# A fused long-convolution and gated-unit backward kernel: every engine's hand-searched order replaced by another one, and one spectrum store issued earlier

## The chip, the cores and the metric

The kernel runs as one program on 1 core of a Trainium2 chip. A core has five engines that run side by side: TensorE (PE, matrix multiplication into the accumulator memory PSUM), VectorE (DVE) and ScalarE (ACT), which do the elementwise work and copy PSUM back to the on-chip memory SBUF, GpSimd (POOL), and SyncE (SP), which here issues nearly all DMAs. Each engine takes its own queue of instructions strictly in order, and waits where a semaphore says that an input isn't there yet. The metric is the device time of one execution, in microseconds (us); less is better.

## The reference

A forward and its gradient. The forward takes x (2048 tokens, 512 channels), normalises it to xn, convolves k with 4 taps, multiplies by v, convolves the product kv with a 2048-long kernel by FFT (length 4096), gates it with xn, and multiplies it by a gated unit with 1376 hidden columns:

```python
def _A_ref(q, k, v, shift_k, ssm_k, ssm_D):
    k_shift = sum(k_pad[:, t:t + S, :] * shift_k[:, ks - 1 - t] for t in range(ks))
    kv = k_shift * v
    y = irfft(rfft(pad(kv)) * rfft(pad(ssm_k)))[:S].astype(bfloat16)
    return q * (y + kv * ssm_D)

def _B_ref(x, w_gate, w_up, w_down):
    return (sigmoid(x @ w_gate) * (x @ w_up)) @ w_down

xn = _layernorm(x)
out = x + _A_ref(xn, k, v, shift_k, ssm_k, ssm_D) * silu(_B_ref(xn, w_gate, w_up, w_down))
```

Ten outputs are asked for: `out`, and for a given `grad_out` the gradients with respect to q, k, v, the 4 taps, `ssm_k` (512 x 2048, called the spectrum's gradient here, `out_5`), `ssm_D`, and the three weights (`out_7`, `out_8`, `out_9`). All is bfloat16 with f32 accumulation.

## The kernel before

The sequence is laid out as 128 partitions x 16 (`NJ`), the 512 channels in 4 groups (`NG`) of 128 for the convolution, and the tokens in 8 pairs of tiles (`NP`) for the gated unit. The code is written as generators, one for each stream of work. Forward: `strG` (gate and up products `gu_gen`, down product `z_gen`), `strK` and `strV` (the FFT of the long kernel and of kv), `strX` (product of the spectra and inverse). Backward: `strZ` (elementwise gradient of the gate), `strD` (`dh_gen`: gradient of the hidden columns; `x_gen`: gradient of xn, which multiplies by the transposed weights `WgT` and `WuT`), then `dW` (the three weight gradients), `frontC` and `backC` (the FFT of the gradient of y, the products with the stored spectra, and two inverses, channel group by channel group).

The FFT is made of two steps. `step1` and `inv1` are matmuls of the whole 128 x 128 array. `step2` and `inv2` are 32-point transforms: they cut the array into 16 pieces of 32 x 32, and one call of `step2` is 16 matmuls, one for each piece; `inv2` makes 32. A third form stands in `backC` (line 1442, "the strip" from here on): for the tap gradients each channel group makes 64 matmuls of 128 x 32 column strips, four strips side by side, all into one accumulator. In a profile the three forms are told apart as 128\*128, 32\*32 and 128\*32; in a list of instructions the output's shape tells them apart (128xN, 32x512 and 32x128). `last_rows` (line 1467) ends the program with five matmuls that leave 4 rows each (128\*4), and two tiny stores.

Nothing is issued while the generators run. `Rec` numbers and records every operation (`add`), 6,118 in all, with its dependences; `emit` (line 522) then issues them by the table `ORDER`: for each engine the list of operation numbers in the order of its queue ("4008+3" stands for 4008 to 4011), and in "moves" the order of all DMAs. An operation that may run on ACT or DVE (a copy out of PSUM, `evac`, or the normalisation in `ln`) runs on the engine whose list has its number. `BANKS` picks the PSUM banks of each accumulator. So each engine's order is written out by hand, down to the single matmul, and every instruction has one line in the profile, 527 (529 after the change), where it is emitted.

Places that matter below: operations 4008 to 4071 and 4631 to 4694 are the strips of channel groups 0 and 1; 5888 to 5891 and 5894 are the matmuls of `last_rows`. On SP, 2478 and 2484 load the transposed `w_gate` and `w_up` (`b_w2`, line 1138), in one DMA each that transposes on its way; 2476 loads a tile of `grad_out`; 5800 is the store of the last channel group's spectrum gradient (`out_5`, line 1437), 512 KB; 5982, 6049, 6083 and 6117 are stores of `out_8`; 5893 and 5896 are the tiny stores of `last_rows`.

Of the kernel before, what the change touches and what calls it, by code (L numbers as in the profile page):

```python
# [37 lines left out]
        943+1 340 458 945+5 341+2 854+7 344 882+7 414+15 397+1 461+7 509+5 399 515+1 712+5 545+7 567+3 563+2 718+1 566  # L38
        720+2 783+10 609+3 601+7 613+3 817+15 863+15 667+2 659 670+3 660+6 674 891+12 1203+6 1158+7 904+2 952+11 988+4
        964 983+2 979+3 986 965 1210 993+5 966+1 999+4 622+3 630+7 626+3 638+3 646+7 642+3 1044+3 1212+15 970+7 1048+3  # L40
        1035+7 1167+2 1089+7 1170+1 1006+7 1172+5 1016+15 1056+10 1100+15 1305+4 1240+15 755+1 751+2 747+3 754 757+5
        771 763 767+3 772+6 764+2 1310+10 1344+15 1190+7 1182+7 1389+14 1362+4 1404 1367+2 844+1 836+7 1429+1 1433+3
        846+2 1431 849+2 920+10 1432 931+4 1509+10 1121+31 1487+6 1338+3 1334+1 1494+3 1617 1336 1259+2 1337 1618+5
        1263+3 1624+8 1262 1235+3 1231+3 1540+15 1070+1 1078+3 1072+5 1082+3 1688+15 1636+7 1276+7 1268+7 1292+7
        1284+7 1644+7 1707+10 1416+7 1408+7 1789+3 1773+1 1439+15 1718+4 1372+15 1775+3 1793 1522+6 1504+2 1766+1 1529
        1500 1794 1501+1 1762+1 1503 1507 1764+1 1795+1 1768+1 1456 1460+3 1457+2 1779 1797+2 1531+7 1854+2 1780+3
        1857+12 1881+5 1568+1 1560+7 1570+5 1887+9 1908+15 1968+5 1828+7 1976+1 1819 1978 1820 1979+2 1974+1 1982+1
        1821+5 2022+10 1666+2 1674+7 1670+3 1669 2033+4 2040+7 1581+31 2139+2 2087+1 2147+5 1872+1 2142 1874+5 2143+3
        2089+4 2153+1 2051 1474+3 1470+1 1478+3 1466+3 1472+1 2052+5 2094+3 2058+3 1726+31 2157+15 1899+7 2192+13
        1837+12 1802+14 2206+1 1850+2 2210 1817 2211+14 1955+7 1947+7 2245+11 2287+2 2257+3 2290+4 2066+2 2074+6  # L50
        2069+1 2081 2071+2 2332+15 2301+3 1994+7 1986+7 2010+7 2002+7 2313+2 2305+2 2371+1 2316+7 2308+3 2373+4 2363+7
        2381+9 2378 2099+31 2391+5 2402+15 2420+9 2175 2236+3 2430+1 2240+3 2183 2228+7 2184 2432+3 2185+1 2176 2441+6
        2177+4 2187 2452 2464+2 2453+1 2182 2467+2 2279 2448 2455 2280+1 2456+3 2282 2188 2274+3 2189 2470+4 2190
        2460+1 2490+4 2462 2495+10 2510+5 2358+3 2353+2 2516 2518+5 2517 2356 2524+1 2485 2479+1 2530+11 2548+1 2486
        2637 2629+5 2638+4 2609+3 2617+6 2577 2613+1 2487 2615 2578 2550 2481 2579+3 2616 2635+1 2624 2583+1 2551+2
        2643+1 2488 2649 2554 2650+1 2482 2652+8 2585 2555+8 2586+6 2748+12 2564 2593 2761 2594+1 2762+1 2565+4 2596
        2704 2768 2705+1 2788 2707 2789 2597+1 2776+1 2790+1 2796 2769+1 2667+6 2797 2771+1 2778 2792+2 2674 2779+4
        2798+1 2675+6 2773+2 2682+4 2708+1 2687+1 2795 2710+14 2891 2883+2 2892+3 2903+1 2835 2905 2886 2906 2887 2725
        2896 2806+2 2888+1 2897+1 2911+4 2907+1 2836+1 2890 2809 2916+1 2838+1 2918 2909+1 2840+13 2923+2 2854 3014
        2926+3 2855+1 3022+4 3015 2810 2930+4 3016+3 2811+1 3020+1 2813+10 3027+2 2824+3 3042 3034+3 2970+8 2941 3062  # L60
        2942+1 3038 3054+2 3043+1 3039 3057+1 3063+1 2979 3045+1 3040 2980 3041 3065 3059 3047 2981 3048+1 2944+5
        3060+1 2982+1 3101 3072 2950+11 2984+4 3147+2 3175+1 3155+1 2989+2 3167+1 3150+1 3169 3152+1 3177+2 3170+3
        3154 3157+5 3073 3180 3174 3102+4 3181+1 3107+1 3074+1 3109+1 3187+1 3076+6 2962 3083+1 3189+8 3085 3322 3198
        3111+1 3086 3205 3113 3206 3274+2 3314 3087 3315 3277 3316 3282 3114 3088 3234+1 3283 3323+1 3115 3284+1 3089
        3317 3278 3207 3318 3090 3286 3279+1 3287 3091+2 3319+1 3288+1 3325 3321 3236 3281 3208 3237+1 3116+4 3294+15
        3209+3 3239+6 3332 3417 3213 3418 3246+1 3397 3425+2 3214 3405+2 3121+1 3248 3419 3333 3420+4 3398+1 3334+1
        3400 3428 3249 3401+3 3408+4 3429+3 3250 3361 3215 3251+1 3573 3253 3216 3574 3362+1 3254 3437+1 3364 3336+1
        3439+5 3217 3445+3 3365 3218+5 3338 3224+2 3366+1 3255 3751 3339+9 3569 3368+6 3575 3570 3528+1 3375+4 3576
        3380+2 3532+1 3822 3534+1 3571 3530 3572 3531 3349+4 3823 3455+8 3519 3547 3464 3543+3 3520 3824 3523 3521+1
        3548+2 3465+11 3825+3 3524+2 3487+21 3752+3 3673+8 3756 3587+7 3579+7 3682+1 3829 3552+7 3699+7 3691+7 3684+4  # L70
        3560+7 3830+7 3843 3757+5 3893+3 3610+7 3602+7 3763+2 3839 3844 3766 3845 3626+7 3618+7 3897+9 3840 3768 3846
        3813 3907 3769+3 3817+2 3814+1 3773 3820 3774+1 3816 3989+2 3908 3992+6 3637+31 3841+1 3999+4 3865+4 4004
        3870+2 4120+5 3714+15 3777+7 3738+7 3730+7 4085+14 4126+3 3793+3 3919+2 3797+3 3922+4 4100 4130+4 4148+1 4135
        3785+7 3915 3911+3 3916+2 3801+7 3848+5 4150+5 3882+2 3856+1 3854 3858 4156+2 3855 3885 3859+1 4078 4165+2
        3861+2 4159 3874+2 4160+3 4168 3943+1 4169 3935 3886+2 3877+4 4184+1 4074+3 4170+1 3889 4186+10 4079+2 4172
        3936 3945+3 3937+5 4173 3949+1 4174+2 3974+1 3982+3 3970+1 3978+1 3972+1 3980+1 3976+1 4177+3 4197+5 4111
        4115+1 4203+2 4106 4137+2 4141 4107 4507 4206 4142 4117 4143+1 4207+1 4508+2 4108 4209+2 4511+3 4118 4212
        4515+2 4140 4102 4112 4518+3 4213+2 4113 4103 4216 4114 4217+8 4104+1 4109 4522 4540+1 4226+12 3932 4542+8
        4239 4268+6 4280+3 4276+3 4008+3 4275 4296+1 4292+2 4298+1 4012+8 4288+2 4021+3 4295 4025+3 4291 4029+42
        4284+3 4240+7 4551+3 3952+10 4555 3963+4 4249+3 4580+15 4303+2 4311+5 4306+3 4317+1 4310 4327+4 4319+3 4332+1  # L80
        4323+3 4334 4700+4 4613 4705+7 4614 4344+11 4340+3 4713+2 4615+3 4719+7 4363+15 4383+1 4379+3 4387+1 4385
        4389+4 4386 4394 4727+7 4454+2 4619+9 4740+11 4458+1 4472+1 4752 4463 4753+1 4474+1 4755 4476 4802 4467+3 4457
        4460+1 4464+2 4803 4477+2 4949+3 4804+13 4953 4398+22 4443+7 4421 4954+19 4489+2 4435+6 4426+1 4442 4428+1
        4422+3 4877+5 4481+4 4883+3 4974 4492 4523 4531+2 4975+3 4887+1 4493 4889 4498 4890 4524 4534+1 4499 4891+1
        4494+2 4979+1 4525+3 4486 4536+1 4487+1 4538 4893+2 4529+1 4896+3 4500 4900+1 4501 4902+6 5040+4 4502+3
        4562+15 5045+8 4558 5054+16 5090+3 5071 4818+7 4775+7 4767+7 4791+7 4783+7 4834+7 5164+1 5094+11 5123+9 5166+1
        5133+5 4631+3 4826+1 4635+3 4830+3 4828+1 4639+55 4859+3 4842+7 4855+3 5168 5282+12 4596+15 5295+2 5169+1
        5299+2 4921+7 4913+7 4937+7 4929+7 4863+7 5171+4 5302+2 5176+3 5197+2 5323+2 5397+4 5326+12 5305+2 5200+12
        5402+7 5308+6 4989 4981+7 4990+1 4993+3 4992 4997+15 5340+6 5500+8 5410+3 5509+1 5347 5414+1 5348 5416+3
        5349+1 5511+2 5432+4 5106 5420+3 5437+3 5107+1 5072 5424+1 5109+1 5080+1 5073+2 5514 5351+2 5111+1 5426+2 5441  # L90
        5113 5442+1 5515 5114+4 5354+1 5444 5082+1 5076 5084+1 5555 5086+1 5077+2 5556 5445+2 5119+2 5018+7 5483+5
        5557 5489+9 5642 5558+7 5365+3 5361+3 5026+7 5377+7 5643+3 5566+2 5647+5 5141 5574+3 5653+3 5578 5152 5144+1
        5657 5153+2 5569+1 5156 5180 5157+2 5146+1 5181 5579 5188+1 5675 5190 5148+3 5182+1 5191+4 5184 5676+11 5185+2
        5369+7 5385+7 5688 5711+7 5580+4 5456+2 5448+1 5459 5450+3 5460+3 5454+1 5464+2 5468 5472+6 5469+2 5467 5479
        5784+2 5719 5585+4 5625+7 5787+7 5689+1 5633+4 5520+5 5528+7 5526+1 5536+2 5544+4 5540+3 5549+1 5539 5551
# [1459 lines left out]
```

## Time and profile before

| | before |
|---|---|
| median of 3 runs | 446.68 us (446.37 to 447.27) |
| the profiled execution's own device time | 447.08 us |
| span of the profiled execution, first to last instruction | 445.2 us |
| granted TensorE clock, mean | 0.997 |
| instructions of TensorE | 4,907 matmuls, each with its weight load |
| DMA | 116.84 MB in 158,245 packets |

The profile gives the busy time of each engine, and a chain: followed back from the last instruction, what released each step. "PEld" is the weight load of a matmul, which is issued by the same sequencer and overlaps the matmuls before it. "idle before" is the time in which an engine stood still just ahead of an instruction, with what ended that wait; "issue" means that it waited for no semaphore that the profile knows.

### The profile page before, as it was taken

What the parts mean: (1) busy time and instruction counts of PE and PEld (TensorE: products, weight loads), DVE (VectorE), ACT (ScalarE), POOL (GpSimd) and SP (SyncE); (2) the same over time, 40 slices, a digit from 0 to 9 for tenths busy, and PEclk for the clock granted to TensorE, in tenths of its full rate; (3) what the DMA queues carried; (4) which work ended last, traced back from release to release, by engine and by line L of the source; (5) the groups of instructions that cost most, each with busy time, mean ns of one, the idle gap of its engine ahead of it and who ended that gap; (6) DMA issues with size and microseconds to landing.
All of it is one profiled execution on the core that took longest, in us unless ns stands there. A gap on an engine that the chain in (4) does not pass through costs nothing.

```text
span 445.2 us, 11512 instructions
## 1 busy us (share of the span) xinstructions
PE 437.9 (98%) x4907; PEld 304.1 (68%) x4907; DVE 402.4 (90%) x624; ACT 287.1 (64%) x359; POOL 23.5 (5%) x48
## 2 busy tenths in 40 slices
PE   8999999999999999999999999999999999999994
PEld 4886686677858677656556655445587887887883
DVE  8899999999978899999999889599998999998992
ACT  7898779798767668597445344365466665556513
POOL 8301020002000000000000000000000000000000
PEclk9999999999999999999999999999999999999998
DMA  8999698489689999978777899789988999899986
GB/s 276 323 365 270 184 377 272 129 326 226 249 260 274 242 214 269 309 257 251 297 199 278 302 326 320 284 215 226 317 219 228 263 206 275 234 242 279 267 242 207
DMA packets 158245, 116.84 MB, mean 262 GB/s; under 512 B 106426, under 2 KB 142322, under 8 KB 157042
## 3 DMA queue, kind: packets, MB, share of 16 engines
q1 hardware_dynamic: 157120, 115.72, 90.4%
q8 instruction: 38, 0.62, 0.6%
q10 hardware_dynamic: 1074, 0.39, 0.4%
q14 instruction: 13, 0.11, 0.1%
HBM read 43.87 MB, written 46.70 MB: 203 GB/s over the span
## 4 chain that ended last, share of the span: by engine, by line
PE 94%; DMA 2%; ACT 1%; DVE 0%; POOL 0%; ACTq 0%; issue 0%; SPq 0%
PE psum L527 94%; DMA slab<-in_B_w_up_dram 2%; DMA slab<-in_A_q_dram 1%; DVE slab L527 0%; ACT slab L527 0%; ACT L527 0%; POOL slab L527 0%; ACTq L1550 0%; ACTq L527 0%; SPq L527 0%
## 5 line engine op out<-in xcount | busy, mean ns | idle before, releaser
L527 PE MATMUL psum<-slab 128*128 128x256 bf16 (+5 forms) x4907 | 437.9, 300 | 1.7 <-DVE slab L527 1.5
L527 PEld LDWEIGHTS <-slab 128*128 128x128 bf16 (+2 forms) x4907 | 304.1, 96 | 135.3 <-issue 30.8
L527 ACT CAST slab<-psum 128x1024 bf16<-128x1024 f32 (+3 forms) x231 | 197.2, 896 | 114.8 <-PE psum L527 94.8
L527 DVE TENSOR_TENSOR slab<-slab 128x1024 bf16<-128x1024 bf16 (+4 forms) x302 | 239.5, 832 | 7.7 <-ACT slab L527 4.6
L527 DVE STREAM_TRANSPOSE slab<-slab 128x1024 f32<-128x1024 f32 x48 | 64.6, 1355 | 4.9 <-ACT slab L527 2.5
L527 ACT ACTIVATE slab<-slab 128x512 bf16<-128x512 bf16 (+5 forms) x57 | 48.0, 881 | 22.3 <-DVE slab L527 22.1
L527 DVE TENSOR_TENSOR slab<-psum,slab 128x512 bf16<-128x512 f32 (+2 forms) x52 | 31.5, 611 | 7.6 <-PE psum L527 5.2
L527 DVE CAST slab<-psum 128x1024 bf16<-128x1024 f32 (+2 forms) x22 | 24.0, 1104 | 9.6 <-PE psum L527 8.8
L527 ACT ACTIVATE slab<-psum 128x512 bf16<-128x512 f32 (+1 forms) x48 | 27.0, 573 | 8.1 <-PE psum L527 7.9
L527 POOL MEMSET slab<- 128x128 bf16 (+3 forms) x10 | 4.5, 452 | 269.8 <-DVE slab L527 166.7
L527 POOL TENSOR_TENSOR slab<-slab 128x2 f32<-128x2 f32 (+3 forms) x11 | 12.9, 1176 | 80.9 <-DVE slab L527 80.8
L527 ACT ACT_TABLE_LOAD x12 | 15.4, 1283 | 1.9 <-PEq L1539 1.7
L527 DVE SCALAR_TENSOR_TENSOR slab<-slab 128x2 f32<-128x2 f32 (+2 forms) x41 | 14.4, 361 | 0.9 <-POOL slab L527 0.8
L527 DVE SCALAR_TENSOR_TENSOR slab<-psum,slab 128x512 bf16<-128x512 f32 x16 | 11.0, 687 | 3.4 <-PE psum L527 2.4
L527 ACT COPY slab<-psum 128x512 bf16<-128x512 bf16 (+2 forms) x11 | 7.9, 742 | 6.1 <-PE psum L527 6.1
L527 DVE BATCH_NORM_STATS2 slab<-slab 128x6 f32<-128x512 bf16 x16 | 10.7, 677 | 1.0 <-DMA slab<-in_A_q_dram 1.0
L527 DVE STREAM_SHUFFLE slab<-slab 128x1024 f32<-128x1024 f32 x8 | 10.5, 1311 | 0.0
L527 DVE TENSOR_SCALAR slab<-slab 128x512 bf16<-128x512 bf16 (+6 forms) x32 | 9.0, 299 | 0.1
L527 DVE COPY slab<-psum 128x1024 bf16<-128x1024 bf16 (+1 forms) x8 | 4.2, 541 | 0.0
L527 POOL TENSOR_SCALAR slab<-slab 128x1 f32<-128x1 f32 (+3 forms) x10 | 3.3, 331 | 0.5
L527 DVE MEMSET slab<- 32x192 uint32 (+3 forms) x10 | 1.5, 160 | 1.2 <-PEq L1539 0.9
L527 DVE BATCH_NORM_AGGREGATE slab<-slab 128x2 f32<-128x6 f32 x16 | 2.5, 165 | 0.0
(14 smaller groups left out, 9.2 us busy)
## 6 DMA issues: line engine op xcount, KB each, us to landing
KVD<-slab SPq DMA_DIRECT2D x16, 512.0 KB, 3.9
slab<-KVD SPq DMA_DIRECT2D x8, 1024.0 KB, 6.2
out_dram<-slab SPq DMA_DIRECT2D x31, 256.0 KB, 4.0
hD<-slab SPq DMA_DIRECT2D x8, 704.0 KB, 5.3
duD<-slab SPq DMA_DIRECT2D x8, 704.0 KB, 4.6
dgD<-slab SPq DMA_DIRECT2D x8, 704.0 KB, 5.7
slab<-in_A_k_dram SPq DMA_DIRECT2D x4, 1024.0 KB, 9.2
slab<-KVD SPq DMA_DIRECT2D x8, 512.0 KB, 5.6
```

The source lines that it names most:

```text
L527: getattr(getattr(self.nc, eng), meth)(*[place(v) for v in a], **{x: place(v) for x, v in k.items()})
```

## The change

The lists of `ORDER` are replaced behind a head that stays (the first 414 matmuls on TensorE, 78 operations on DVE, 45 on ACT, 32 DMAs on SP), and 35 of the 353 entries of `BANKS`. No operation is added or taken out: TensorE has 4,907 matmuls before and after, SP 232 DMAs. What changes is where each stands, and for 23 operations the engine: 14 go from DVE to ACT (9 copies out of PSUM, 5 normalisations), 9 from ACT to DVE (7 copies, 2 normalisations); ACT has 14 instead of 12 table loads. The search that gave the new lists counted a price for each change of the array's form (128\*128, 32\*32, 128\*32), and the store of the last spectrum gradient was afterwards moved up in SP's list by hand.

```diff
@@ ORDER["tensor"], the strip of channel group 0 (4008 to 4071)
-        4239 4268+6 4280+3 4276+3 4008+3 4275 4296+1 4292+2 4298+1 4012+8 4288+2 4021+3 4295 4025+3 4291 4029+42
+        4105 4008+63 4268+25 4296 4294+1 4297+2 4580+9 4551+2 4590+4 3952+6 4595 4613+1 4249+3 4554+1 3960+1 3959
...
@@ ORDER["tensor"], the end
-        5889 5969 6064+17 6104+2 5970+3 6107+8 5974+5 5894 5890+1
+        5971+1 6036+2 6097+1 5781 6039+2 6061 5973 6099+16 6042+5 6062+19 5974+5 5888+3 5894
...
@@ ORDER["sync"], the end
-        5356 4761 5710 5213 5709 5901 5900 4756 5732 5939 5980 6049 6083 6117 5982 5800 5896 5893
+        5572 5356 5710 4561 5709 5901 5900 5213 5732 4756 5939 5980 5800 6049 6117 6083 5982 5893 5896
```

The queue of TensorE in the strip of channel group 0 (32x128 is a matmul of the strip, 32x512 one of a 32-point transform), before:

```order
L527 MATMUL psum<-slab 32x128
L527 LDWEIGHTS slab
L527 MATMUL psum<-slab 32x512
L527 LDWEIGHTS slab
L527 MATMUL psum<-slab 32x128
```

And after, where the strip ends:

```order
L529 LDWEIGHTS slab
L529 MATMUL psum<-slab 32x128
L529 LDWEIGHTS slab
L529 MATMUL psum<-slab 32x512
L529 LDWEIGHTS slab
```

Before, the 64 matmuls of this strip stand in five pieces (4, 9, 4, 4 and 43), with pieces of 32-point transforms of 15, 8, 3, 1, 1 and 4 matmuls around and between them (32 in all); after, the 64 stand in one piece, and the 32 behind them in one piece. The strip of channel group 1 goes from pieces of 4, 4 and 56, with 2, 6 and 16 transform matmuls between and behind, to 64 and 24. Counted over the whole queue of TensorE, the form changes 126 times before and 107 times after. All of the difference stands behind the 2,500th matmul: six visits to the 32 x 32 form ahead of the strip of group 0, of 16, 16, 32, 40, 16 and 24 matmuls, become five, of 32, 32, 32, 32 and 16; and the five matmuls of `last_rows`, which stood in pieces of 1, 1 and 3, are one piece at the end. Ahead of the 2,500th the visits are the same in number and size.

The queue of SP around the transposing loads of the two weights, before (hD and zD are scratch buffers in DRAM, slab is the SBUF):

```order
L527 DMA slab<-in_B_w_up_dram 128x4x96
L527 DMA slab<-in_A_q_dram 128x1024
L527 DMA_TRANSPOSE slab<-in_B_w_gate_dram 128x10x512
L527 DMA hD<-slab 128x2816
L527 DMA out_dram<-slab 128x1024
L527 DMA_TRANSPOSE slab<-in_B_w_up_dram 128x10x512
```

And after:

```order
L529 DMA slab<-zD_74 128x512
L529 DMA slab<-in_B_w_up_dram 128x4x96
L529 DMA_TRANSPOSE slab<-in_B_w_gate_dram 128x10x512
L529 DMA hD<-slab 128x2816
L529 DMA out_dram<-slab 128x1024
L529 DMA slab<-in_grad_out_dram 128x1024
L529 DMA_TRANSPOSE slab<-in_B_w_up_dram 128x10x512
```

A load of 256 KB from `grad_out` has come in between the two transposing loads, and between the transposing load of `w_down`, a few rows above, and that of `w_gate` there are three more transfers than before (a store of 512 KB to the spectra's scratch and two loads of 128 KB from zD). On TensorE the first matmul that needs the transposed `w_up` is the 2,027th of the queue before, and the 2,015th after.

The end of SP's queue, before (4x512 and 4x128 are the tiny stores of `last_rows`, 128x2048 is the store of the last spectrum gradient):

```order
L527 DMA out_dram<-slab 128x8x256 x2
L527 DMA out_dram<-slab 128x4x256
L527 DMA out_dram<-slab 128x2x96 x2
L527 DMA out_dram<-slab 128x4x256
L527 DMA out_dram<-slab 128x2048
L527 DMA out_dram<-slab 4x128
L527 DMA out_dram<-slab 4x512
```

And after:

```order
L529 DMA out_dram<-slab 128x8x256 x2
L529 DMA out_dram<-slab 128x2048
L529 DMA out_dram<-slab 128x4x256
L529 DMA out_dram<-slab 128x2x96 x2
L529 DMA out_dram<-slab 128x4x256
L529 DMA out_dram<-slab 4x512
L529 DMA out_dram<-slab 4x128
```

The store of 128x2048 (5800) stood third from last and now stands ahead of the last four stores of `out_8`; the two tiny stores have changed places.

More of the change, by code (lines that the diff above doesn't have):

```diff
@@ L148 @@
         56+1 29 87 30 63 92 88 38 34 89 98 91 86 99 90 117 100+1 118 103+2 107+1 106 109 81 110 144 102 111+1 119 229
-        503 914 1328 937 1659 1931 2263 3538 4758
+        503 1328 914 937 1659 1931 2263 3538 4758
     """,
     "sync": """
[10 rows of a table removed]
[10 rows of a table added]
     """,
@@ L176 @@
 BANKS = (
-    "32210312000322012001011110100010000101120100101000011101011001001001132011100001100001011101011003011011001011"
-    "00001111101021010101010100100101010011000110101001101000101110032120101012310101321010101020100231010110023001"
-    "01011100021210100101020211003211232031020230221302320122120210211012013202223331021223102102121300120131010301"
-    "21031001012102101301321"
+    "13312002113312112001011110100010000101100300101000011101011001021001032011100001100001011101011003011011001011"
+    "00001111101021010101010100100101010001000110101001101000101112032132101012310101321010101013100321010110123001"
+    "01011100021210100201010211003211232231020230221302321122120210211012013232202331021223102102121300120031010301"
+    "21031001011102110301321"
 )
```

236 rows, old and new, of the table ORDER are left out of this document.

## The prediction

> **What bounds the kernel now.** I read the busy table first, then the middle of the span by windows, then the chain, then what TensorE's weight loads wait for.
>
> ```profile
> PE 437.9 (98%) x4907; PEld 304.1 (68%) x4907; DVE 402.4 (90%) x624; ACT 287.1 (64%) x359; POOL 23.5 (5%) x48
> ```
>
> The first row is the whole span of 445.2 us; the next has the stretch from 20 to 440 us (its length, then busy time and count for PE, PEld, DVE, ACT, POOL, then the granted clock, the DMA share and GB/s). The third is the piece of the chain that begins at 19.95 us and lasts 419.37 us.
>
> ```profile
> 20.00:440.00 420.00, 419.67 (x4744) 291.77 (x4743) 385.84 (x576) 270.46 (x340) 10.05 (x10) 1.00 0.92 262
> ...
> 19.95 419.37 PE psum L527 x4741
> ```
>
> TensorE has a matmul in flight for 419.67 of 420 us, at a clock of 1.00, and the chain stays on it without a break for 419.37 us. No engine and no transfer stands in for it. So the time is the 20 us of start, TensorE's queue, and the stores behind it. TensorE's work is the same before and after, matmul by matmul, so in that stretch only two things can change the time: pauses between matmuls that no wait explains, and new waits. The pauses are seen in the weight loads:
>
> ```profile
> PEld L527 <- issue: 27.4, 100, 0.4
> PEld L527 <- DVE slab L527: 2.6, 7, 0.4
> ```
>
> These are idle us, how often, and the longest, between 20 and 440 us. The weight loads stood still 100 times with no semaphore to wait for, 27.4 us in all, and only 7 times, 2.6 us, for DVE. Not all of the 27.4 us is lost: part of it lies under matmuls that still stream. What a pause costs has to be read where the array's form changes.
>
> **The strips of channel groups 0 and 1.** The timeline of weight loads around the strip of group 0 (start, length, form, count, idle before):
>
> ```profile
> 333.94 0.13 PEld L527 LDWEIGHTS <-slab 32*32 32x32 bf16 x15
> 334.30 0.28 PEld L527 LDWEIGHTS <-slab 128*32 128x32 bf16 x12 [0.23 <-issue]
> 334.81 0.37 PEld L527 LDWEIGHTS <-slab 128*32 128x32 bf16 x12 [0.23 <-issue]
> 335.40 0.26 PEld L527 LDWEIGHTS <-slab 128*32 128x32 bf16 x5 [0.23 <-issue]
> 335.88 0.26 PEld L527 LDWEIGHTS <-slab 128*32 128x32 bf16 x5 [0.23 <-issue]
> 336.37 0.82 PEld L527 LDWEIGHTS <-slab 128*32 128x32 bf16 x47 [0.23 <-issue]
> 337.42 0.67 PEld L527 LDWEIGHTS <-slab 128*128 128x128 bf16 x12 [0.23 <-issue]
> ```
>
> The counts add up to 96: the strip's 64 and 32 transform matmuls (a row takes in the few of the other form behind it). They occupy 337.42 - 333.94 = 3.48 us. And the strip of group 1, with its end as the price of one undivided:
>
> ```profile
> 373.21 0.26 PEld L527 LDWEIGHTS <-slab 128*32 128x32 bf16 x6 [0.21 <-issue]
> ...
> 374.20 1.03 PEld L527 LDWEIGHTS <-slab 128*32 128x32 bf16 x72 [0.23 <-issue]
> 375.45 0.55 PEld L527 LDWEIGHTS <-slab 128*128 128x128 bf16 x6 [0.23 <-issue]
> ```
>
> Here 64 and 24 matmuls take 375.45 - 373.21 = 2.24 us, but the last 72 of them (56 of the strip in one piece, then 16 of the transform) only 1.25 us. The transform visits, and the strip of a later group that already stands in one piece:
>
> ```profile
> 297.25 0.14 PEld L527 LDWEIGHTS <-slab 32*32 32x32 bf16 x16 [0.42 <-issue]
> 297.61 0.87 PEld L527 LDWEIGHTS <-slab 128*128 128x128 bf16 x7 [0.23 <-issue]
> ...
> 304.97 0.19 PEld L527 LDWEIGHTS <-slab 32*32 32x32 bf16 x32 [0.42 <-DVE slab L527]
> 305.55 1.09 PEld L527 LDWEIGHTS <-slab 128*128 128x128 bf16 x8 [0.39 <-issue]
> ...
> 308.87 0.56 PEld L527 LDWEIGHTS <-slab 32*32 32x32 bf16 x40 [0.42 <-issue]
> 309.65 3.78 PEld L527 LDWEIGHTS <-slab 128*128 128x128 bf16 x19 [0.23 <-issue]
> ...
> 316.27 0.16 PEld L527 LDWEIGHTS <-slab 32*32 32x32 bf16 x24 [0.42 <-issue]
> 316.83 1.11 PEld L527 LDWEIGHTS <-slab 128*128 128x128 bf16 x11 [0.39 <-issue]
> ...
> L527 PE MATMUL psum<-slab 128*32 128x128 bf16 x64 | 1.1, 220 | 0.0
> ```
>
> From a visit's first weight load to the first of the next form: 0.36 us for 16, 0.58 for 32, 0.78 for 40, 0.56 for 24. A strip of 64 in one piece is busy for 1.1 us, so eight more strip matmuls cost 8 x 1.1/64 = 0.14. After the change group 0 is 64 and 32 in two pieces: 1.25 + 0.14 + (0.58 - 0.36) = 1.61 instead of 3.48, **-1.87 us**. Group 1 is 64 and 24: 1.25 + 0.14 + (0.56 - 0.36) = 1.59 instead of 2.24, **-0.65 us**. The other way of adding, 1.1 + 0.58 and 1.1 + 0.56, gives -1.80 and -0.58; that is the bound on the low side.
>
> **The six visits ahead of them, and the last rows.** Before 16, 16, 32, 40, 16, 24: 3 x 0.36 + 0.58 + 0.78 + 0.56 = 3.00 us. After 32 four times and 16: 4 x 0.58 + 0.36 = 2.68, so -0.32. One entry goes as well; its pause is 0.42 us where the way back has 0.23, under the last whole-array matmul for the most part, so between 0 and 0.19; I take 0.1: **-0.42 us**. `last_rows` goes from three pieces (1, 1, 3) to one. Its form shows this pause:
>
> ```profile
> 439.23 0.14 PEld L527 LDWEIGHTS <-slab 128*4 128x4 bf16 x3 [0.21 <-issue]
> ```
>
> Two visits fewer save at least two entries, 0.42, and at most entries and ways back, 2 x (0.21 + 0.23) = 0.88; part of that is hidden under 128-row matmuls, so I stay near the lower end: **-0.45 us**. The form changes make **-3.39 us** in all, between -2.8 (1.80, 0.58, 0.32 and 0.42, less 0.3 for what the neighbours may hide) and -3.9 (1.87, 0.65, 0.51 and 0.88).
>
> The Trainium skill (TensorEngine Tiling (Array Packing), Tiling Modes, Key Properties) says that a change of tiling mode drains TensorE, which the pauses of 0.21 to 0.42 us at every change bear out. By the drain of about 128 cycles that TensorE: Matmul & The Clock Gate (Step-by-step: what each phase is for) in the Trainium skill states, 53 ns at 2.4 GHz, 19 changes fewer would be an estimate of 1.0 us only; the rows of the two strips alone show 2.52, so the rows decide.
>
> **The end.** The last copies on ACT, and SP's last stores:
>
> ```profile
> 439.34 1.05 ACT L527 CAST slab<-psum 128x512 bf16<-128x512 f32 x2 [0.28 <-PE psum L527]
> ...
> 440.37 1.46 SPq L527 DMA_DIRECT2D out_dram<-slab  x3
> ...
> 440.96 0.87 SPq L527 DMA_DIRECT2D out_dram<-slab  x2
> ```
>
> Here the 512 KB store 5800 is issued at 440.37, and the two tiny stores only from 440.96 on, though ACT was done at 439.34 + 1.05 = 440.39. Moved ahead of the stores of `out_8`, 5800 is issued while SP waits for copies, and its transfer runs while those are still made; the tiny stores come 440.96 - 440.37 = 0.59 us earlier. Next in line is the copy on ACT, so no more than that can go: **-0.55 us**, between -0.45 and -0.59.
>
> **The transposing load of `w_up`.** This is the wait I expect in exchange. SP's timeline, the load's time to landing, and how many matmuls TensorE had begun by two moments:
>
> ```profile
> 166.59 8.87 SPq L527 DMA_TRANSPOSE slab<-in_B_w_up_dram  x1
> ...
> 180.46 0.46 SPq L527 DMA_DIRECT2D slab<-in_grad_out_dram  x1
> ...
> slab<-in_B_w_up_dram SPq DMA_TRANSPOSE x1, 12.4
> ...
> 0.00:178.50 178.50, 176.78 (x2017) 128.42 (x2018) 163.55 (x255) 143.50 (x182) 22.03 (x46) 1.00 0.92 266
> 0.00:180.07 180.07, 178.35 (x2026) 129.35 (x2027) 165.09 (x257) 145.07 (x184) 22.03 (x46) 1.00 0.92 266
> ```
>
> Before, the load is issued at 166.59 and lands 12.4 later, at 179.0; its first user is the 2,027th matmul, at 180.1, so 1.1 us to spare. After, the first user is the 2,015th, which TensorE reaches before 178.5, at about 178.3 if the matmuls ahead are the same mixture, and up to 178.8 if more of them are long; I take 178.55. And a load of 256 KB stands ahead of it on SP, which costs 0.46 us of issue. Landing at 179.0 + 0.46 against 178.55: **+0.9 us**, between 0 (SP is through earlier) and 1.4. TensorE's queue is in order, so everything behind that matmul waits too.
>
> **Other waits.** All lists are new, so other operands may come late. The 7 waits for DVE, 2.6/7 = 0.37 us each, are the nearest row: half of one more is **+0.2**, which I take, one fewer -0.3, four more +1.5. The 23 operations that change engine, and two more table loads on ACT, are covered as long as ACT has its 445.2 - 287.1 = 158 us of idle time:
>
> ```profile
> L527 ACT ACT_TABLE_LOAD x12 | 15.4, 1283 | 1.9 <-PEq L1539 1.7
> ```
>
> Two more are 2.6 us of ACT; uncovered they would fall into the same +1.5. DVE at 90% loses five operations on balance, so it comes no later.
>
> **Sum.** -3.39 - 0.55 + 0.9 + 0.2 = -2.84 us. The profiled execution took 447.08 (445.2 of span and 1.9 around it), which makes 444.24; the median of the runs, 446.68, lies 0.4 lower, and so does the forecast: **443.8 us**.
>
> **Rivals.**
> - The waits take most of the gain. DVE is busy for 385.84 of the 420 us, so an order that serves one wait can make another; 2.0 to 2.8 us more of small waits than I count give 445.8 to 446.7, no change that can be measured. Against it: all of the queues up to the 2,500th matmul keep their visits, and only 7 waits stand there today. Chance 0.09.
> - Slower, by DMA. Ahead of the transposing loads stand three more transfers (512 KB to the spectra's scratch, two of 128 KB) and the 256 KB already counted, 1,024 KB. The DMA engines are nearly full:
>
> ```profile
> DMA packets 158245, 116.84 MB, mean 262 GB/s; under 512 B 106426, under 2 KB 142322, under 8 KB 157042
> ```
>
>   If nothing else is put back for them, 1.02 MB at 262 GB/s delay the weights by 3.9 us and the issue by 0.46: 4.4 in all, a landing at 183.4, and TensorE stands for 4.8 us instead of 0.9. Then -3.39 - 0.55 + 0.2 + 4.8 = +1.1, **447.7 us**. It decides from a shift of 4.2 us on. Against it: the program moves the same bytes in all, so what comes earlier leaves its old place to others, and the DMA share of 0.92 in the rows above leaves some room. Chance 0.08.
> - TensorE isn't what bounds. Then the pauses that go are filled again by waits for DVE and DMA at once, and the time stays at 446.7 less at most the end's 0.55. The Trainium skill (Perfetto Trace Analysis, Identifying the Most-Contended Engine) calls matmul busy time a bad measure and would look at the weight loads, busy for 68% here, below DVE's 90%. Against it stands the chain of 419.37 us on TensorE and 7 waits in it. Chance 0.03.
>
> **How the numbers follow.** Forecast 0.80, rivals 0.09, 0.08, 0.03. Two tenths of a per cent, 0.9 us, is about what a measurement of this kernel can tell from no change, so faster means under 445.8 and slower over 447.6. The best sum is -3.9 - 0.59 + 0 - 0.3 = -4.8 (441.9), the worst -2.8 - 0.45 + 1.4 + 1.5 = -0.35 (446.3), which is the first rival already. All bounds at once at the good end are unlikely, so the range is 442.2 to 446.3; it takes in the greater part of the first rival.
>
> **What would show it.** Right, if: the strips of groups 0 and 1 stand in one row of 64 each of about 1.1 us; the weight loads' pauses with "issue" behind them are some 19 fewer; SP's last issue begins within 0.6 us of ACT's last copy; TensorE has one wait of 0.5 to 1.4 us near 178 us for the transposed `w_up`. Wrong, if the strip stands in one row and the span hasn't become shorter by about as much at the same matmul, if waits of PE for DMA or DVE add up to more than 2 us, or if the load of `w_up` lands after 181 us.

## The result and the profile after

The changed kernel takes 444.52 us (median of 17 runs, 443.45 to 447.71) beside 446.9 us for the kernel before (17 runs, 446.34 to 449.01): a ratio of 0.9949, with a 95% interval of 0.9934 to 0.9965, or 2.3 us less (1.6 to 2.9). The forecast was 443.8 against 446.68, 2.84 less. The sign and the range held; the gain was half a microsecond smaller. In a second comparison the same changed kernel (a_again, below) gained less: 0.997, or 1.3 us (0.4 to 2.3).

The profiled execution took 445.0 us with a span of 443.2. First the busy table, and the stretch from 20 to 440 us, as they were shown of before (38 matmul records are missing from this trace; the weight loads are all there):

```profile
PE 432.0 (97%) x4869; PEld 303.2 (68%) x4907; DVE 398.5 (90%) x619; ACT 294.9 (67%) x366; POOL 21.8 (5%) x48
...
20.00:440.00 420.00, 414.46 (x4712) 291.39 (x4749) 382.34 (x572) 279.11 (x348) 8.41 (x10) 1.00 0.94 263
```

The clock is the same, TensorE is still the engine that is nearly never idle, and the wait that the forecast named is there. What TensorE and its weight loads waited for between 20 and 440 us (idle us, how often, longest):

```profile
PEld L529 <- issue: 27.4, 90, 1.3
PEld L529 <- DVE slab L529: 3.2, 9, 0.7
PE psum L529 <- ACT slab L529: 1.1, 1, 1.1
PE psum L529 <- DMA slab<-in_B_w_up_dram: 1.0, 1, 1.0
```

Before there were 100 pauses with "issue" behind them, now 90, and 1.3 us of one is the wait for `w_up` seen a second time, at the weight load. The forecast said some 19 fewer. It took every change of form to have a pause, but 18 changes before and 7 after show none of more than 0.15 us in this view, every way out of a strip among them, so most of the 19 had none to lose. The wait for ACT, which ends at 20.39 us, belongs to the start of the program; the wait for the DMA is new. The timeline of weight loads where the strips stand now:

```profile
336.23 1.27 PEld L529 LDWEIGHTS <-slab 128*32 128x32 bf16 x88
337.89 0.10 PEld L529 LDWEIGHTS <-slab 128*128 128x128 bf16 x1 [0.38 <-issue]
...
372.99 1.17 PEld L529 LDWEIGHTS <-slab 128*32 128x32 bf16 x88 [0.21 <-issue]
374.55 0.99 PEld L529 LDWEIGHTS <-slab 128*128 128x128 bf16 x13 [0.39 <-issue]
```

Group 1's strip and its 24 transform matmuls take 374.55 - 372.99 = 1.56 us, where they took 2.24 and the forecast said 1.59. Group 0's 64 and 32 run without a row between too. The window cuts their row off on the left: the first of these weight loads is at 336.17, so they take 337.89 - 336.17 = 1.72 us, where they took 3.48 and the forecast said 1.61.

**Where the time went.** To compare two orders of the same 4,907 matmuls, I gave each matmul the step that its form and its neighbours have in the trace of before (0.216 us for 512 columns, 0.109 for 256, the ways in and out of a form by their rows), and took these off the times at which the weight loads really start. What remains at a matmul is the time waited up to there. Counting from the 251st matmul leaves the start of the program out. "Sum" is the change of the span without the start, and the three columns add up to it:

| against the kernel before | steps of TensorE's queue | waits | end, behind the last weight load | sum |
|---|---|---|---|---|
| changed kernel | -3.48 | +2.00 | -1.10 | -2.58 |

The 2.00 of waits are 1.15 at the 2,015th matmul (`w_up`), 0.48 of small ones ahead of it, 0.28 behind it, and 0.1 at the very end, where the visits of `last_rows` turn out cheaper than their steps. In this execution the program also started 0.50 us later, so the spans (445.24 and 443.16) differ by 2.1 and not 2.6.

### The profile page after: what moved, and what is told of

The parts are those of the page before. It is cut to its first block, busy times and chain, and to the rows that moved or that the text cites. A ratio compares the mean times of both kernels' runs of the same rounds, so it can differ in the third digit from the quotient of the medians.

```text
span 443.2 us, 11480 instructions
## 1 busy us (share of the span) xinstructions
PE 432.0 (97%) x4869; PEld 303.2 (68%) x4907; DVE 398.5 (90%) x619; ACT 294.9 (67%) x366; POOL 21.8 (5%) x48
## 4 chain that ended last, share of the span: by engine, by line
PE 86%; DMA 6%; DVE 4%; issue 1%; ACT 1%; POOL 0%; ACTq 0%; SPq 0%; DVEq 0%
PE psum L529 86%; DMA slab<-in_B_w_up_dram 4%; DVE slab L529 4%; DMA slab<-KVD 1%; ACT slab L529 1%; DMA slab<-in_A_q_dram 1%; ACT L529 0%; POOL slab L529 0%; ACTq L529 0%; SPq L529 0%; DVEq L529 0%
## 5 line engine op out<-in xcount | busy, mean ns | idle before, releaser
L529 PE MATMUL psum<-slab 128*128 128x256 bf16 (+5 forms) x4869 | 432.0, 299 | 6.6 <-DVE slab L529 1.8
L529 ACT CAST slab<-psum 128x1024 bf16<-128x1024 f32 (+3 forms) x234 | 200.3, 899 | 123.5 <-PE psum L529 110.4
L529 ACT ACTIVATE slab<-slab 128x512 bf16<-128x512 bf16 (+5 forms) x60 | 51.0, 879 | 11.3 <-DVE slab L529 11.1
L529 DVE CAST slab<-psum 128x1024 bf16<-128x1024 f32 (+2 forms) x19 | 20.4, 1081 | 11.5 <-PE psum L529 11.2
L529 POOL TENSOR_TENSOR slab<-slab 128x2 f32<-128x2 f32 (+3 forms) x11 | 11.2, 1027 | 80.5 <-DVE slab L529 80.4
L529 DVE TENSOR_SCALAR slab<-slab 128x512 bf16<-128x512 bf16 (+6 forms) x29 | 7.7, 287 | 0.1
L529 DVE COPY slab<-psum 128x512 bf16<-128x512 bf16 (+1 forms) x9 | 4.6, 528 | 0.0
```

The lines of the kernel that those rows point to most:

```text
L529: getattr(getattr(self.nc, eng), meth)(*[place(v) for v in a], **{x: place(v) for x, v in k.items()})
```

## Experiments

Each kernel is either the kernel before or the changed one with one piece of its order edited (a_again is the changed one as it is); nothing is left out of the computation. The times are medians, the ratio is to runs of the kernel before on the same chip, and the last columns are the sums of the trace, made as above, so from one execution each. "Against" is the kernel from which it was made.

| kernel | us | ratio (95%) | against | steps | waits | end | sum |
|---|---|---|---|---|---|---|---|
| b_strips | 445.65 | 0.998 (0.9959 to 1.0) | before | -2.58 | +1.13 | 0.0 | -1.46 |
| b_strip1 | 446.62 | 0.9984 (0.9972 to 0.9996) | before | -0.69 | 0.0 | 0.0 | -0.69 |
| b_cut | 448.12 | 1.0015 (0.9998 to 1.0032) | before | +1.25 | +0.09 | 0.0 | +1.36 |
| b_rows | 446.05 | 0.998 (0.997 to 0.999) | before | -0.47 | +0.10 | -0.24 | -0.61 |
| b_store | 445.74 | 0.9977 (0.996 to 0.9995) | before | 0 | 0.0 | -0.93 | -0.94 |
| a_resplit | 448.54 | 1.0039 (1.0018 to 1.006) | changed | +2.58 | +1.21 | 0.0 | +3.81 |
| a_resplit2 | 446.73 | 0.9991 (0.9973 to 1.0009) | changed | +1.76 | -0.14 | 0.0 | +1.65 |
| a_up | 444.24 | 0.9933 (0.9911 to 0.9956) | changed | 0 | -0.72 | 0.0 | -0.69 |
| a_up2 | 444.39 | 0.9939 (0.9915 to 0.9963) | changed | 0 | -0.32 | 0.0 | -0.32 |
| a_up3 | 444.33 | 0.9928 (0.9911 to 0.9945) | changed | 0 | 0.0 | 0.0 | +0.06 |
| a_again | 445.81 | 0.997 (0.9949 to 0.999) | changed | 0 | +0.22 | 0.0 | +0.27 |
| a_dist | 443.91 | 0.9927 (0.99 to 0.9953) | changed | 0 | -0.86 | +0.06 | -0.80 |

### The strips by themselves: b_strips, b_strip1, b_cut

```diff
b_strips, kernel before, tensor (and the strip of group 1 likewise)
- 4239 4268+6 4280+3 4276+3 4008+3 4275 4296+1 4292+2 4298+1 4012+8 4288+2 4021+3 4295 4025+3 4291 4029+42 4284+3
+ 4239 4008+63 4268+6 4280+3 4276+3 4275 4296+1 4292+2 4298+1 4288+2 4295 4291 4284+3
```

> The kernel before, with only the strips of channel groups 0 and 1 put in one piece each and their 32 and 24 transform matmuls in one piece behind (13 form changes fewer, no other engine's list touched). Forecast's theory (a form change costs TensorE its pause): 2.5 us less, 444.2 against 446.7, with bounds of 2.0 and 2.8. Rival, TensorE isn't what bounds: the pauses fill up with waits, 446.7, no change. Rival, a change costs only a drain of some 50 ns: 0.7 us less, 446.0.

Only 0.9 us of the 2.5 came out by the ratio (0 to 1.8), 1.46 by the trace. The steps are there to the full; what spoils them are two new pauses behind the strip of group 0, in the timeline of weight loads:

```profile
334.83 0.11 PEld L536 LDWEIGHTS <-slab 32*32 32x32 bf16 x8 [0.49 <-issue]
...
337.63 1.89 PEld L536 LDWEIGHTS <-slab 128*96 128x96 bf16 x20 [0.68 <-ACT slab L536]
```

The second pause, at a matmul of 128 x 96, is a wait for ACT by the row: this matmul now comes earlier than its input. The first stands within the transform matmuls, and no row shows a releaser for it, so its cause stays open. So closing the gaps is not enough: what ACT must deliver behind the strip has to come earlier as well. The changed kernel has neither pause: strip and transforms of group 0 take 1.72 us there and 2.00 here, and no wait of this size stands behind them.

```diff
b_strip1, kernel before, tensor: group 1 alone
- 4631+3 4826+1 4635+3 4830+3 4828+1 4639+55
+ 4631+63 4826+1 4830+3 4828+1
```

> The kernel before, with only the strip of channel group 1 in one piece (64, then its 24 transform matmuls; 4 form changes fewer). The same with both strips gained 1.2 us where 2.5 were expected, and its trace shows 1.1 us of new waits behind the strip of group 0 and none behind that of group 1. So the full 0.65 us should be left here: 446.2 against 446.9, and no new wait in the trace between 373 and 380 us. Rival, each strip's gain is halved by new waits: 0.3 us less. With 50 ns for each change: 0.2 us less.

0.69 us less by the trace, with no wait between, and the times agree (0.9984, 0.7 us). The step of the forecast that said 0.65 is right where nothing waits.

```diff
b_cut, kernel before, tensor: the strip of group 2
- 5215+63 5946+5
+ 5215+7 5946 5223+7 5947 5231+7 5948 5239+7 5949 5247+7 5950 5255+7 5951 5263+15
```

> The kernel before, with the strip of channel group 2 (one piece of 64 there) cut into seven pieces, a single whole-array matmul of the weight gradients (5946 to 5951, taken from right behind it) between each two: 12 form changes more, nothing else moved. By the price that the rows of the strips give (2.5 us for 13 changes) 2.3 us more; by the steps of a lone matmul in the trace (a way into the strip 0.09 us, a way out 0.15 less the ordinary step) 1.2 us more, 448.1 against 446.9. Rival, 50 ns for each change: 0.6 us. Rival, TensorE isn't what bounds: no change.

Twelve changes more cost 1.36 us of span, 0.11 each, and 0.7 us by the ratio, whose interval reaches from nothing to 1.4. The trace is nearest to the 1.2 of a lone matmul's steps: a change between strip and whole array costs less than one between strip and 32-point transforms, for which b_strip1 has 0.69/4 = 0.17 and a_resplit2, below, 1.65/8 = 0.21.

### The strips put back: a_resplit, a_resplit2

```diff
a_resplit, changed kernel, tensor: pieces as before
- 4008+63 4268+25 4296 4294+1 4297+2
+ 4268+14 4008+3 4283+7 4012+8 4291+2 4021+3 4296 4025+3 4294 4029+42 4295 4297+2
```

(written as runs of numbers; group 1 likewise)

> The changed kernel, with the strips of groups 0 and 1 cut again into the pieces of before (4, 9, 4, 4, 43 and 4, 4, 56, with 15, 8, 3, 1, 1, 4 and 2, 6, 16 transform matmuls around and between). Forecast's theory: 2.5 us more, 447.0 against 444.5. If the waits of the new order have slack to lose because TensorE isn't what bounds: no change, 444.5. With 50 ns for each change: 0.7 us more, 445.2.

It cost 3.81 us by the trace, more than the steps, and the ratios (1.0039 against 0.9949) agree. The surplus stands at the first piece of transforms, in the timeline of weight loads and in that of matmuls:

```profile
335.33 0.11 PEld L538 LDWEIGHTS <-slab 32*32 32x32 bf16 x9
336.50 0.10 PEld L538 LDWEIGHTS <-slab 32*32 32x32 bf16 x6 [1.06 <-issue]
...
336.50 7.84 PE L538 MATMUL psum<-slab 32*32 32x512 bf16 x163 [0.76 <-ACT slab L538]
```

By these rows ACT's copy is made under the strip when the strip is in front. The next kernel asks whether that is all:

```diff
a_resplit2, changed kernel, tensor: group 0 only, strip in front
- 4008+63, then 32 transforms
+ 43 of the strip, 4 transforms, 4, 1, 4, 1, 4, 3, 9, 23
```

> The changed kernel, with only the strip of channel group 0 cut again, and so that its first piece stands ahead of the transform matmuls (43, 4, 4, 4, 9 of the strip, with 4, 1, 1, 3, 23 of the transforms behind them; 8 form changes more). Cut as before, with 15 transform matmuls first, it cost 1.2 us more than its form changes, and the trace showed the transforms waiting for a copy by ACT. Theory: the strip in front is also the cover under which that copy is made; with 43 of the strip in front the wait is gone, and only the changes are paid, 8 x 0.21 = 1.7 us more than the changed kernel: 446.2. Rival, cutting makes such a wait wherever it is done: 447.2 or more.

1.65 us more by the trace, with no wait at this place, as expected. The times show 0.9 us (446.73, and 445.81 for the changed kernel in that comparison) with intervals that overlap, so the size rests on the trace. So the strip in one piece and in front serves twice: 0.2 us for each change saved with the transforms, and a cover of 1.2 us for a copy.

### The last rows and the last store: b_rows, b_store

```diff
b_rows, kernel before, tensor: end
- 5888 6062+1 6047 5889 5969 ... 5974+5 5894 5890+1
+ 6062+1 6047 5969 ... 5974+5 5888+3 5894
b_store, kernel before, sync and moves
- 5980 6049 6083 6117 5982 5800 5896 5893
+ 5980 5800 6049 6083 6117 5982 5896 5893
```

> The kernel before, with only the five matmuls of last_rows in one piece at the end of TensorE's queue. Forecast's theory: 0.45 us less by two visits fewer, 446.4 against 446.9. Rival, the visits cost little and the last five now stand later in the queue than the copies behind them want: no change or up to 0.2 us more.

> The kernel before, with only the store of the last spectrum gradient moved ahead of the last four stores of out_8. Forecast's theory: the two tiny stores come 0.59 us earlier, 0.55 us less, 446.1 against 446.7. From the profile after, whose end is 1.0 us shorter behind the last weight load: if all of that is the store, 1.0 us less, 445.7. Rival, the end is set by the landing of the last bytes whatever the issue order: 446.7.

b_rows gains 0.61 by the trace, 0.37 of it on TensorE and 0.24 behind its last weight load. b_store gains 0.93 at the end, where the forecast had 0.55. ACT's last copies and SP's last three issues there:

```profile
438.97 1.05 ACT L536 CAST slab<-psum 128x512 bf16<-128x512 f32 x2 [0.28 <-PE psum L536]
...
439.58 1.18 SPq L536 DMA_DIRECT2D out_dram<-slab  x3
```

SP is done at 440.76, 0.74 us after ACT (440.02). Before it was done at 441.83, 1.44 after ACT (440.39). That is 0.70 and not 0.59, as the tiny stores themselves are issued faster; the other 0.23 lie behind the last issue, which ended 3.41 us before the span's end before and ends 3.18 before it here. That the transfer of 512 KB, which then is no longer under way beside the tiny ones, makes this last part was not tried.

### The load of `w_up`: a_up, a_up2, a_up3, a_again, a_dist

```diff
a_up and a_up3, changed kernel, sync and moves
- 2478 2300 2299 2476 2484
+ 2478 2300 2299 2484 2476
a_up2
+ 2478 2300 2484 2299 2476
```

> The changed kernel, with the transposing load of w_up issued ahead of the 256 KB load of grad_out again (one exchange in SP's list). The forecast charged that load 0.46 us; TensorE waits 1.0 us for w_up in the profile after. Theory A, the wait follows the load's place in the queue: 0.5 us less, 444.0 against 444.5, and the wait is 0.5 us. Theory B, the load is late mostly because the stores ahead of it are late: the issue moves by 0.5 but the landing doesn't, and the time stays at 444.5. Theory C, grad_out is late in turn: more than 444.5.

> The changed kernel, with the transposing load of w_up ahead of the store of out as well as ahead of the 256 KB load of grad_out, so issued some 2 us earlier than in the changed kernel. With the exchange alone the wait for w_up was gone from the trace, and 0.4 of its 1.15 us came back as two small waits 20 us later. If that is all there is, the same again: 0.7 us less than the changed kernel, 443.8 against 444.5, and no wait for w_up. Rival, the store of out or the load of grad_out is now late for its own user: 444.5 or more.

In a_up's trace the wait is gone, and 0.4 us come back as two small waits at 202 and 207 us. In a_up2 it is gone too, and 0.8 come back, one of them a wait for a transposing load of SBUF (0.8 us), which now is late. So far theory A, by one trace each. But the same kernel as a_up, once more, had the wait again:

> The changed kernel with the transposing load of w_up ahead of the load of grad_out, once more beside the changed kernel, to settle whether the 0.7 us that its trace shows are there in the times: 443.8 against 444.5, every start of the kernel taken together. Rival, what the trace shows is one execution's luck: no difference between the two.

> The changed kernel itself, beside the next one on the same chip: 444.5.

Waits of TensorE between 150 and 215 us in a_up3:

```profile
PE psum L538 <- DMA slab<-in_B_w_up_dram: 1.0, 1, 1.0
```

Its program had started 0.67 us earlier than a_up's, and TensorE stood all the same, from 178.68 us on. What differs can be read from the landing events in the traces, 16 for each such load. In a_up all 16 of `w_up` come within 0.2 us, the last at 177.51. In a_up3 fifteen have come by 178.24, and the last only at 179.77. A sixteenth event some 1.5 us behind the others stands in 11 of the 14 traces, in the kernel before (177.49, then 179.00) and the changed one (179.40, then 180.86) too; a_up, a_up2 and b_store have none. In all five traces with the wait, fifteen events had come before TensorE got there: it stood for the sixteenth alone. What makes that one late was not tried.

In the times, a_up3 lies 1.5 us below a_again beside it on the same chip (444.33 and 445.81, with intervals that don't overlap). The traces don't put that down to the load: both have the wait, and of the 2.6 us between their spans 2.4 stand ahead of the 251st matmul. Whether the exchange saves anything by itself stays open. How long the whole way of the weights is, the timeline of SP shows, in the changed kernel:

```profile
160.63 5.79 SPq L529 DMA_TRANSPOSE slab<-in_B_w_gate_dram  x1
166.47 0.57 SPq L529 DMA_DIRECT2D hD<-slab  x1
...
168.75 0.43 SPq L529 DMA_DIRECT2D slab<-in_grad_out_dram  x1
169.28 8.00 SPq L529 DMA_TRANSPOSE slab<-in_B_w_up_dram  x1
```

The chain of the changed kernel at the same place (start, us, what):

```profile
160.93 8.35 PE psum L529 x64
169.28 11.59 DMA slab<-in_B_w_up_dram
180.91 0.38 PE psum L529
```

And SP in the kernel before:

```profile
159.14 5.59 SPq L527 DMA_TRANSPOSE slab<-in_B_w_gate_dram  x1
164.79 1.23 SPq L527 DMA_DIRECT2D hD<-slab  x1
```

The transposing load of `w_gate` overwrites the straight weights, so it starts when their last user, matmul 2443, is through (in all 14 traces SP issues it 0.4 us after 2443's weight load, wherever that stands); that of `w_up` follows on the same queue, and TensorE needs it in turn. This detour is tied to TensorE at both ends and lasts 180.91 - 160.63 = 20.3 us in the changed kernel, and 166.59 + 12.4 - 159.14 = 19.9 before. By the steps of its queue TensorE had 21.2 us of work between 2443 and the first user of `w_up` before, and has 19.4 after. So 1.1 us to spare became a wait of 1.15 mostly by the distance on TensorE, 1.8 us less, and by 0.4 of a longer detour, in which SP's one load more (0.53 us from its issue to the next) has a part. Without the late sixteenth event the detour of the changed kernel would be 179.40 - 160.63 = 18.8 us, and there would be no wait.

```diff
a_dist, changed kernel, tensor
- 2585+6 2649 2592+5 2650+10 2557+4 (around the first user, 2588)
+ 2585+2 2649+11 2557+1 2588+9 2559+2
```

> The changed kernel with SP's lists untouched, and 14 matmuls that do without w_up (2649 to 2660, 2557, 2558; 1.7 us of TensorE) put ahead of its first user, 2588. Theory: the transposing load of w_gate overwrites weights whose last matmul is 2443, the load of w_up follows it on SP, and both together last 20.3 us from there; the kernel before had 21.2 us of TensorE's work between 2443 and the first user of w_up, the changed one has 19.4. With 21.1 the wait is gone: no wait for w_up in the trace, whatever the start of the execution, and 0.7 to 1.15 us less than the changed kernel: ratio to before 0.9925 (443.6), where the small waits that followed in an earlier run take back up to 0.4. Rival, the load is late because of DMA traffic at its time, not because of its distance: the wait stays at about 1 us, ratio 0.995.

SP in this kernel, with its lists as in the changed one:

```profile
160.59 6.57 SPq L538 DMA_TRANSPOSE slab<-in_B_w_gate_dram  x1
...
170.37 7.24 SPq L538 DMA_TRANSPOSE slab<-in_B_w_up_dram  x1
```

The load is issued at 170.37, 1.1 us later than in the changed kernel, its sixteenth event comes late again, at 181.21 (180.86 there), and TensorE, at its first user at about 181.5, doesn't wait for it. So 14 matmuls of distance take the wait away. The rival as it was put falls, but a landing that is fixed in time, whatever TensorE does, isn't told apart by this run: the first user moved by 1.7 us, more than the wait, so such a landing would have been in time too. The trace gains 0.80 us (1.15 less the small waits that follow), and the ratio to before is 0.9927. Against the changed kernel that is no more than a tendency, as the intervals overlap.

## Why the prediction was right

Point by point, with the forecast beside what the runs showed:

| term | forecast | measured | from |
|---|---|---|---|
| form changes | -3.39 | -3.4 (steps -3.48, less 0.1 at `last_rows`) | after, b_strip1, a_resplit2, b_rows |
| end | -0.55 | -1.10 | after; b_store -0.93 |
| wait for `w_up` | +0.9 | +1.15 | after, a_again, a_dist |
| other waits | +0.2 | +0.75 | after |
| sum | -2.84 | -2.58 in the trace, -2.3 (1.6 to 2.9) in the times | |

- **What bounds.** That TensorE's queue sets the time was right: changes of the order on TensorE come out as their steps in b_strip1, b_cut and a_resplit2, with less than 0.15 us of waits on either side. The rival by which removed pauses refill at once falls as a whole. b_strips shows where it holds in part: 1.13 of 2.58 us came back.
- **The price of a change of form.** 0.17 to 0.21 us between strip and 32-point transforms, 0.11 between strip and whole array. That six visits became five was not tried by itself; b_strips and b_rows leave 0.43 us of the steps for it, where the forecast had 0.42. The drain that the Trainium skill states (TensorE: Matmul & The Clock Gate, Step-by-step: what each phase is for), by estimate 53 ns, is half to a quarter of that, so the runs don't agree with it as a price.
- **The end** was mis-sized: I let only SP's issue time go, 0.59 us, and said that no more could go as ACT is next. That part came: the first tiny store is issued 0.57 us behind ACT's last copy before, and 0.02 in b_store. The tiny stores' own issue and the time behind the last issue became shorter as well, and the last matmuls of `last_rows` in one piece gave 0.24 behind the last weight load, which I had not looked for there.
- **The wait for `w_up`** was right in place and about right in size, but the size is luck: two errors cancel. I let its landing move by 0.46 us, from 179.0 to 179.5; it came at 180.9, since the load of `w_gate` ahead of it was issued 1.49 us later. And I had TensorE there at 178.55; it came at 179.8 (180.91 less 1.15), with the 0.5 us later start and 0.5 us of small waits in front. The quantity that decides, the distance on TensorE between the last user of the old weights and the first of the new ones (21.2 and 19.4 us), can be read from the two orders, and I had not read it. Nor had I seen that 1.5 us of the 12.4 to landing belong to one landing event of sixteen, which is not late in every execution.
- **Other waits** were mis-sized, 0.75 for 0.2, though inside the bound. Two pieces, of 0.26 and 0.28 us, are the largest. The first is at 131 us, where the chain of the changed kernel leaves TensorE for a load of stored spectra and DVE behind it. The second is at 318.3 us, at the end of 16 us in which the chain is mostly on DVE; a pause at the same matmul stands in seven of the eight traces of the changed order. Rows of the chain at both places:

```profile
124.10 5.05 DMA slab<-KVD
129.25 0.99 DVE slab L529
...
301.69 1.24 DVE slab L529
...
317.01 1.24 DVE slab L529
```

  The page of the changed kernel has 86% of the chain on TensorE, that of the kernel before 94%: in these places the new order has nothing to spare. What would take these waits away wasn't tried.
- **The slower rival**, a delay of both weights by the transfers put ahead of them, is not what the traces show. `w_gate` is issued 0.41 us behind 2443's weight load in both, so the three transfers ahead of it don't hold up its issue. Of the 2.7 us by which `w_up` is issued later (169.28 for 166.59), 1.5 are the later 2443 (0.5 of them the start), and 1.2 stand on SP between the two loads, with the 256 KB load among them. The rival needed 4.2.
- **Two of its signs of being wrong** were nearly met: `w_up` lands at 180.9 where 181 was the limit, and waits of all kinds add up to 2.00 us where 2 for DMA and DVE was.

Three terms were too small, the waits by 0.25 and 0.55 and the end by 0.55. They partly balance, so it is in part luck that the total is nearer than its parts.

## What to carry to other kernels

Where one engine is busy throughout, a change of its order is worth the sum of its own steps, and they can be had from the rows of the old trace; but what stands behind the shortened place must arrive earlier too, so the gain of a lone edit (b_strips) is smaller than that of the same edit in an order that was fitted around it. Where a load overwrites an operand, look for both of its ends on the busy engine, the last user of the old and the first user of the new contents, and compare the work between them with the duration of the detour. A load is through when its last landing event has come: the 1.5 us between the fifteenth and the sixteenth made the wait here. And one trace is not a verdict on a wait of about 1 us whose neighbours are DMAs: the same kernel had it and had it not.

## What was not expected of the hardware

The start of the program differs between executions of the same first instructions. Up to the 251st matmul the kernels' first 414 matmuls and 32 DMAs on SP are the same, yet it is reached up to 2.6 us apart. The chain shows where: a load of `w_up` at 9 us, from its issue to what waits for it, in the kernel before, in the changed one and in a_again:

```profile
9.38 6.81 DMA slab<-in_B_w_up_dram
```

```profile
9.25 7.38 DMA slab<-in_B_w_up_dram
```

```profile
9.87 8.05 DMA slab<-in_B_w_up_dram
```

This alone is as large as half of what the change brings. The changed kernel's own runs lie between 443.45 and 448.47 us in two comparisons, with medians of 444.52 and 445.81; why they spread more than a microsecond was not settled.
